# A down product between scores and state reads in every cell, the next first blocks loaded later, and two steps of y exchanged, in a fused mLSTM cell and GELU block

## The chip, the cores and the metric

The kernel runs on one core of one Trainium2 chip. The metric is the device time of one execution in microseconds (us), from which the median of several runs is taken. The engines are TensorE (PE: matmuls and transposes into PSUM, with its weight loads PEld), VectorE (DVE), ScalarE (ACT), GpSimd (POOL) and SyncE (SP, which here issues every data DMA).

## The reference

Two blocks follow each other. The first is a recurrence for batch 4, 8 heads, 768 positions and a head width of 40, cut here to what matters:

```python
for t in range(S):
    m_new = np.maximum(f_gate[:, :, t] + m, i_gate[:, :, t])
    f_stab, i_stab = np.exp(f_gate[:, :, t] + m - m_new), np.exp(i_gate[:, :, t] - m_new)
    C = f_stab * C + i_stab * outer(v[t], k[t])          # state, 40 x 40 a head
    n = f_stab * n + i_stab * k[t]
    y[:, :, t] = sigmoid(o_gate[t]) * (C @ q[t]) / max(|n . q[t]|, 1)
```

Its output, as 3072 rows of 320, goes into the second block: `h = x @ w_in` (320 x 2048), an exact GELU, and `g @ w_out` (2048 x 320). Everything is float32.

## The kernel before, in words

The 768 positions are cut into six chunks of 128 (`NCH`, `L`). For each chunk a **cell** computes the recurrence in its parallel form for the four batches b = 0 to 3: scores k·q by PE (`ps`, L505 and L521), multiplied by decay weights W that ACT makes with an exponential (L433) from a broadcast of M (loaded at L175 and L178, masked by POOL at L407); reads of the carried state (`pf`, L576), the update of the state from k and weighted v (L583, DVE and POOL around it), and the values W·v (`ph`, L615). The sum of state reads (`far`) and values is gated, divided by its denominator (`finish`, the y step, L628 to L633) and turned by PE transposes into the columns of x (`turn_y`, L650); `split_x` makes the parts that the up product wants (L668, L669). The turn reads two blocks of 128 columns from `ob` and the last 64 from `y_rest`, a copy that DVE makes at L639 (`twice`), one buffer for all batches.

The **up** stage of a chunk multiplies x by w_in in three float parts (L810, L821), and ACT applies GELU into `g` (L825). The **down** stage is `g @ w_out` in a seven-product form with sums of weights and of hidden blocks (`down_steps`): 14 steps F, each of 16 recorded matmuls at L886. Steps 1 and 2 are `p1`, 3 and 4 `p6`, 5 and 6 `p2`, 7 and 8 `p5`, 9 and 10 `p7`, 11 and 12 `p3`, 13 and 14 `p4`; after each second one ACT copies or DVE adds the bank into the output tile (L899), and `p3` and `p4` send it out (L853).

The order of the work is written out by hand. Chunk 0 and cells 0 and 1 are in a list FRONT. Then, for c = 1 to 5, the up stage of chunk c is followed by its down stage, in which cell c+1 runs; the text calls this **stage c**. The order inside it is the list DOWN for c = 1 to 3, LAST_CELL for c = 4 (DOWN with the two passes changed), and 14 plain F for c = 5. The letters: M mask, W weights, G gate, S `scores_two` (two batches), C `carry_two` (state reads and update), V values, Y finish, X `turn_y`, R `split_x`, L and B loads for the last batch, K and Q `turn_k` and `turn_q`, D its weighted values, F one down step, Z one step of the weight sums of chunk 1, N the late hidden sums (L916). Each engine executes its own instructions in the order in which the list issues them; S, C and V of two batches are called a **pass** here, so each stage has two.

In cells 2 and later k and q come as small 32 x 32 blocks, 16 loads for one batch (`load_blocks`, L158), into one buffer `blocks`, and DVE transposes them (L456). A batch's blocks are loaded when those of the batch before it are turned:

```python
def turn_q(self, b):
    self.turn_half(b, 1)
    n = self.c * B + b + (1 if b < B - 2 else 2)
    if b < B - 1 and n < NCH * B:
        load_blocks(n, by_block)
```

so Q2 loads the first batch of the next cell; the fourth batch has its own buffer inside `g`. K0, Q0, K1 and Q1 of the next cell are issued inside the next up stage. The values of a batch then issue the loads of M (L178), k and v (L146, L148) for a later one, and `turn_y` that of the o gate (L148). SP issues all of these in list order, and waits where a buffer isn't free.

## Time and profile before

| | us |
|---|---|
| median of 3 runs | 484.55 |
| the runs | 481.93, 484.55, 487.79 |
| the profiled execution | 484.29 |
| its span, first to last instruction | 482.5 |
| PE busy | 472.3 (98%) |
| PEld busy | 412.2 (85%) |
| DVE busy | 345.2 (72%) |
| ACT busy | 222.2 (46%) |
| POOL busy | 70.7 (15%) |
| down stages 1, 2, 3 and 4 | 43.7, 46.4, 43.8, 41.8 |

Times inside the kernel are counted from the first instruction. The stages are read as stretches of the timeline: 158.2 to 201.9, 230.6 to 277.0, 305.7 to 349.5 and 378.2 to 420.0. Stage 4 has less work than the others, as the last cell doesn't update the state (no L583). A float32 matmul shows as two records. Matmuls are pipelined and their ends are modelled, so lengths of PE work are best taken from start to start. "issue" names time in which an engine waited for nothing that the profile shows.

### The profile page before, as it was taken

To read this page: it belongs to the slowest core of one execution; us is meant where nothing else is said; L and a number is where in the kernel's file an instruction comes from. 1 tells how busy PE (TensorE), PEld (TensorE's weight loads), DVE (VectorE), ACT (ScalarE), POOL (GpSimd) and SP (SyncE) were. 2 spreads that over 40 slices of the span, in tenths; PEclk is the share of its full clock that TensorE was granted. 3 is DMA by queue.
4 is the path that set the end of the run, shared out by engine and by line. 5 is a ranking of instruction groups with operands and counts; after the bars stand their busy time and mean duration, and the time that the engine had idled before them with its cause. 6 is when DMAs were issued, how large, how long until landed. Compare 5 with 4: busy or idle time off the path is not lost.

```text
span 482.5 us, 11952 instructions
## 1 busy us (share of the span) xinstructions
PE 472.3 (98%) x4740; PEld 412.2 (85%) x4740; DVE 345.2 (72%) x762; ACT 222.2 (46%) x477; POOL 70.7 (15%) x104
## 2 busy tenths in 40 slices
PE   8899999999999999999998999999999999999997
PEld 7787888877777999977998977899977899977997
DVE  7899689797879898747596767398867488724321
ACT  6977999844532941122941104862104862112300
POOL 3001210000020233200333200135100114000000
PEclk9999999999999999999998999999999999999999
DMA  9998966379320364931264921255931250100001
GB/s 174 201 216 179 188 170 151 84 192 208 113 29 6 39 123 66 205 71 17 34 133 63 201 53 21 33 95 95 197 70 19 33 88 8 46 10 0 1 1 54
DMA packets 170423, 44.49 MB, mean 92 GB/s; under 512 B 156448, under 2 KB 163904, under 8 KB 170368
## 3 DMA queue, kind: packets, MB, share of 16 engines
q1 hardware_dynamic: 170368, 43.73, 46.6%
q8 instruction: 37, 0.61, 0.5%
q14 instruction: 18, 0.15, 0.1%
HBM read 39.58 MB, written 4.13 MB: 91 GB/s over the span
## 4 chain that ended last, share of the span: by engine, by line
PE 88%; DVE 6%; SPq 1%; ACT 1%; DMA 1%; issue 1%; DVEq 0%
PE po L886 31%; PE pu L810 21%; PE po L863 7%; PE pu L755 6%; PE pu L821 6%; PE ph L615 5%; PE ps L521 2%; PE pu L761 2%; PE pf L576 2%; PE px L650 2%; PE pf L583 1%; PE ps L505 1%; SPq L148 1%; PE pt L479 1%; ACT g L825 1%
## 5 line engine op out<-in xcount | busy, mean ns | idle before, releaser
L886 PE MATMUL po<-w_out,g 128*128 128x160 f32 x640 | 91.3, 300 | 0.0
L886 PEld LDWEIGHTS po<-w_out,g 128*128 128x128 f32 x640 | 87.8, 190 | 1.9 <-ACT g L825 1.8
L825 ACT ACTIVATE g<-pu 128x512 f32<-128x512 f32 x80 | 40.8, 614 | 53.4 <-PE pu L821 53.3
L886 PE MATMUL po<-w_sums,sums 128*128 128x160 f32 x320 | 48.7, 307 | 0.0
L886 PEld LDWEIGHTS po<-w_sums,sums 128*128 128x128 f32 x320 | 45.5, 195 | 0.5
L660 ACT ACTIVATE x_hi<-px 128x384 fp32r<-128x384 f32 x20 | 9.8, 489 | 69.3 <-PE px L650 69.3
L810 PE MATMUL pu<-x_hi,w_in_hi 128*128 128x512 f32 x160 | 41.7, 402 | 0.0
L742 DVE TENSOR_TENSOR sums<-g 128x512 f32<-128x512 f32 x20 | 13.8, 689 | 38.6 <-ACT g L825 38.6
L810 PE MATMUL pu<-x_lo,w_in_lo 128*128 128x512 f32 x160 | 40.6, 395 | 0.0
L433 ACT ACTIVATE W<-W,aT 128x128 f32<-128x128 f32 x128 | 39.2, 388 | 0.1
L810 PEld LDWEIGHTS pu<-x_hi,w_in_hi 128*128 128x128 f32 x160 | 28.5, 188 | 9.3 <-ACT g L825 4.1
L810 PEld LDWEIGHTS pu<-x_lo,w_in_lo 128*128 128x128 f32 x160 | 30.1, 188 | 7.2
L863 PE MATMUL po<-w_out,g 128*128 128x320 f32 x128 | 35.2, 433 | 0.0
L863 PEld LDWEIGHTS po<-w_out,g 128*128 128x128 f32 x128 | 24.0, 190 | 9.5
L810 PE MATMUL pu<-x_all,w_in_mid 128*128 128x512 f32 x80 | 31.7, 396 | 0.1
L825 ACT ACT_TABLE_LOAD x5 | 6.4, 1283 | 55.1 <-PE pu L821 41.3
L810 PE MATMUL pu<-x_all,w_mid 128*128 128x512 f32 x80 | 31.7, 396 | 0.0
L899 DVE TENSOR_TENSOR o_sb<-po,o_sb 128x320 f32<-128x320 f32 (+1 forms) x27 | 12.5, 463 | 25.9 <-PE po L886 21.9
L407 POOL TENSOR_SCALAR_AFFINE_SELECT W<-W 128x1024 f32<-128x1024 f32 (+2 forms) x20 | 21.9, 1103 | 61.7 <-DMA W<-M_d 54.2
L755 PE MATMUL pu<-first_x,w_in 128*128 128x256 f32 x128 | 29.1, 382 | 0.0
L445 POOL MEMSET g<- 32x1024 f32 x8 | 7.6, 945 | 135.1 <-ACT W L433 134.8
L755 PEld LDWEIGHTS pu<-first_x,w_in 128*128 128x128 f32 x128 | 23.8, 190 | 3.4 <-DVE w_in L375 0.4
(183 smaller groups left out, 901.6 us busy)
## 6 DMA issues: line engine op xcount, KB each, us to landing
W<-M_d SPq DMA_DIRECT2D x16, 512.0 KB, 5.2
bits<-in_moe_w_in_dram SPq DMA_DIRECT2D x20, 256.0 KB, 4.3
bits<-in_moe_w_out_dram SPq DMA_DIRECT2D x16, 320.0 KB, 3.4
ob<-in_o_gate_dram SPq DMA_DIRECT2D x24, 160.0 KB, 3.8
out_dram<-o_sb SPq DMA_DIRECT2D x24, 160.0 KB, 1.9
vb<-in_v_dram SPq DMA_DIRECT2D x14, 160.0 KB, 5.1
kb<-in_k_dram SPq DMA_DIRECT2D x14, 160.0 KB, 5.2
g<-M_d SPq DMA_DIRECT2D x4, 512.0 KB, 4.5
```

Source lines behind the costliest of these rows:

```text
L407: nc.gpsimd.affine_select(out=x, in_=x, compare_op=OP.is_ge, fill=1.0e30, base=base, pattern=[[0, H], [1, x.shape[2]]], channel_multiplier=-1)
L433: nc.scalar.activation(out=W[n][:, h, :], in_=src, func=AF.Exp, scale=-1.0, bias=aT[:, self.c, r:r + 1])
L615: nc.tensor.matmul(ph[r, h, :], Pm[:, h, r], vb[turn_of(n)][:, h, :], start=True, stop=True)
L660: nc.scalar.activation(out=parts["x"][:, :, t], in_=px, func=AF.Copy, scale=PART)
L742: nc.vector.tensor_tensor(out=s1, in0=a21, in1=a22, op=OP.add)
L755: nc.tensor.matmul(banks[-1][e][:, i - i0, :], in_tile(i, x)[:, e, i % 2 * P:(i % 2 + 1) * P], first_x[:, x, t0:t1], start=(x == 0 and i = ...
L810: nc.tensor.matmul(pus[i][e], w[k][:, e, i * P:(i + 1) * P], x[:, k, :], start=(n == 0 and k == 0), stop=False, skip_group_check=True)
L821: nc.tensor.matmul(pu[e], w[r, i // 2, i % 2 * P:(i % 2 + 1) * P], x[r, NX, :], start=False, stop=(n == 2), skip_group_check=True)
L825: nc.scalar.activation(out=g.t[:, HF * e + i, :], in_=pu[e], func=AF.Gelu, scale=4097.0)
L863: nc.tensor.matmul(po[b], g.t[:, f, b * L:(b + 1) * L], w_out[:, f, :], start=(f == 0), stop=(f == NF - 1))
L886: nc.tensor.matmul(bank[at][:, i, :], lhs(j, t), rhs(j), start=(first and i == 0 and j == 0), stop=(i == n - 1 and j == HF - 1), skip_grou ...
L899: nc.vector.tensor_tensor(out=to, in0=pb, in1=x, op=OP.add)
```

## The change

Three edits of the list, and one of the code that it calls.

In DOWN the pair "F S0" becomes "S0 F", and "S2 C2 V2 V3 F" becomes "S2 F C2 V2 V3": one down step stands between the scores and the state reads in both passes. LAST_CELL, which had these two already, goes away, and stage 4 uses DOWN.

The loads of the next cell's first blocks leave `turn_q` (Q2) and become a step of their own, `j`, issued after the values V3. In stage 4 it does nothing, as before.

"Y3 X1" becomes "X1 Y3": the second turn of y is issued before the fourth y is finished, in stages 1 to 4.

```diff
 DOWN = """
-    M0 Z M1 W0 F L3 F B3 W1 Z Z F S0 K2 C0 M2 G0 G1 G2 G3 V0 V1 W2 F Q2 K3 Q3 Y0 M3 D3 F F W3 F S2 C2 V2 V3 F Z N F Y1
-    X0 R0 Y2 F F Y3 X1 R1 F X2 R2 F X3 R3 F"""
-LAST_CELL = DOWN.replace("F S0", "S0 F").replace("S2 C2 V2 V3 F", "S2 F C2 V2 V3")
+    M0 Z M1 W0 F L3 F B3 W1 Z Z S0 F K2 C0 M2 G0 G1 G2 G3 V0 V1 W2 F Q2 K3 Q3 Y0 M3 D3 F F W3 F S2 F C2 V2 V3 j Z N F Y1
+    X0 R0 Y2 F F X1 Y3 R1 F X2 R2 F X3 R3 F"""
...
         def turn_q(self, b):
             self.turn_half(b, 1)
-            n = self.c * B + b + (1 if b < B - 2 else 2)
-            if b < B - 1 and n < NCH * B:
-                load_blocks(n, by_block)
+            if b < B - 2:
+                load_blocks(self.c * B + b + 1, by_block)
             if self.c < NCH - 1 and b < B - 1:
                 self.weigh_values(b)
+
+        def load_next(self):
+            if self.c + 1 < NCH:
+                load_blocks((self.c + 1) * B, by_block)
...
-            steps = cell_steps(c + 1, "MWGTscVYXRLKQDCBS", g)
+            steps = cell_steps(c + 1, "MWGTscVYXRLKQDCBSj", g)
...
-        play("F " * 14 if c + 1 == NCH else LAST_CELL if c + 2 == NCH else DOWN, steps)
+        play("F " * 14 if c + 1 == NCH else DOWN, steps)
```

## The prediction

> **What bounds the kernel now.** I read the page first, for the engine that sets the end. These are its busy line and its chain of waits by engine.

> ```profile
> PE 472.3 (98%) x4740; PEld 412.2 (85%) x4740; DVE 345.2 (72%) x762; ACT 222.2 (46%) x477; POOL 70.7 (15%) x104
> ...
> PE 88%; DVE 6%; SPq 1%; ACT 1%; DMA 1%; issue 1%; DVEq 0%
> ```

> TensorE (PE) is the bound: 98% busy and 88% of the chain. So an edit is worth only what it changes in PE's own sequence: a hole taken away, or a costlier order of the same matmuls. Next I cut the time into the four down stages in which a cell of the recurrence runs (stage c multiplies chunk c down while cell c+1 is computed). Columns: stretch, length, PE, PEld, DVE, ACT and POOL busy, granted clock, DMA share, GB/s.

> ```profile
> 158.20:201.90 43.70, 43.24 (x687) 42.58 (x685) 37.80 (x97) 19.91 (x50) 14.62 (x19) 1.00 0.59 102
> 230.60:277.00 46.40, 44.92 (x687) 44.22 (x686) 35.04 (x80) 19.90 (x50) 15.33 (x20) 0.96 0.59 108
> 305.70:349.50 43.80, 43.28 (x687) 42.51 (x685) 35.11 (x80) 19.87 (x50) 14.96 (x18) 1.00 0.62 110
> 378.20:420.00 41.80, 41.80 (x623) 40.78 (x622) 33.66 (x76) 19.91 (x50) 9.15 (x9) 1.00 0.25 41
> ```

> Stages 1 to 3 do the same PE work (687 matmuls), yet stage 2 takes 2.6 us more than stage 3, at a lower clock. Stage 4, which already runs with a down product between scores and state reads, has no hole at all. So I followed PE through the second score pass of stage 2 in the timeline (start, length, line, tiles, count).

> ```profile
> 251.61 1.57 PE L521 MATMUL ps<-qT,kT 64*64 64x128 f32 x64
> 253.00 1.09 PE L576 MATMUL pf<-state,qT 64*64 64x41 f32 x64
> 254.03 1.13 PE L583 MATMUL pf<-vw,kb 128*64 128x41 f32 x32
> 254.98 1.11 PE L615 MATMUL ph<-vb,W 128*64 128x41 f32 x32
> 255.91 0.29 PE L615 MATMUL ph<-vb,g 128*64 128x41 f32 x2
> 257.68 1.39 PE L615 MATMUL ph<-vb,g 128*64 128x41 f32 x30 [1.48 <-issue]
> 259.00 3.79 PE L886 MATMUL po<-w_sums,sums 128*128 128x160 f32 x16
> 262.62 2.34 PE L886 MATMUL po<-w_out,g 128*128 128x160 f32 x16
> ```

> Two losses stand here: 1.48 us in which PE waited for nothing that the profile shows, and a down product of 3.79 us where its neighbour takes 2.34. The windows give the second its reason (clock 0.50), and the DMA view of two short windows (251 to 254, then 254.9 to 256.4) hints at the first.

> ```profile
> 259.00:261.80 2.80, 2.80 (x11) 2.80 (x11) 0.50 (x1) 0.00 (x0) 1.89 (x3) 0.50 0.24 26
> ...
> q1 hardware_dynamic: 1651, 0.74, 107.1%
> ...
> q8 instruction: 1, 0.02, 5.0%
> ```

> From 251 to 254 the data queue fills all 16 DMA engines (107.1%) and no instruction packet runs. The next one, 16 KB on q8, starts at 255.04 and takes 1.21 us. Since the one before it (244.50) PE had been issued 432 instructions; over the whole trace the spacing is about 256. So the fetch was some 170 instructions late, and PE ran dry at 255.97. One pass of scores (L521), state reads (L576), state update (L583) and values (L615) is about 450 instructions in 5.4 us; a down product (L886) is 32 in 2.2 us. Only in the pass can 256 instructions be used up in about 3 us.

> [...] Here PEclk is 0.50 right behind the hole, for 3.41 us from 258.37 in the trace; the idle part was only 1.48 us[...].

> **The change part by part.**

> *A down product between scores and state reads (stages 1 to 3, twice each; stage 4 has it already).* No matmul is added; PE changes over between small and dense matmuls more often. Stage 4 shows the new order:

> ```profile
> 382.72 1.57 PE L521 MATMUL ps<-qT,kT 64*64 64x128 f32 x64
> 384.22 2.44 PE L886 MATMUL po<-w_sums,sums 128*128 128x160 f32 x16
> 386.59 1.14 PE L576 MATMUL pf<-state,qT 64*64 64x41 f32 x64
> 387.66 2.06 PE L615 MATMUL ph<-vb,W 128*64 128x41 f32 x64
> ```

> Start to start, the first pass of stage 2 with its seven products is 230.56 to 251.61: 6.72 (three products) + 1.39 + 1.02 + 0.96 (L583) + 2.07 + 8.89 (four products) = 21.05 us. In stage 4 it is 4.55 + 1.50 + 2.37 + 1.07 + 1.99 + 8.90 = 20.38 without L583; with its 0.96 it is 21.34, or 21.42 with stage 2's 2.07 for the values. So the split costs 0.29 to 0.37, say 0.33 us a pass: six passes, +2.0 us. From below it could be nothing, if some is taken up elsewhere; from above 0.38, so 0 to 2.3.

> What it takes away, in this execution: in stage 1 the first values take 168.28 to 170.95 = 2.67 us with 0.46 of "issue", against 2.07: 0.60. In stage 2 the second values take 254.98 to 259.00 = 4.02 against 2.05 in stage 3: 1.97; the product behind them 3.62 start to start against 2.28: 1.34. Together 3.9 us. With the product between, the 256 instructions that ran dry in stage 2 have 2.3 us more to arrive in, against the 1.48 that were missing; in stage 1 the same[...]. The wait of the DVE for scores doesn't appear as a cost: W is multiplied (L527, 3.1 us for two cells' tiles) before the values start, today as well.

> The moved score pass waits for nothing new: it starts 2.2 us earlier, and its banks were released by the last gelu at 232.73 in stage 2, before 235.05. The second weights (ACT, done at 239.15) then hold DVE's second half by about 1 us, as stage 4 shows (0.73 idle), but the values that need it start at 242. The add of the eighth product (L899, 0.49 us) now stands ahead of the state reads' work on DVE, and its product is done by then.

> *The next first blocks loaded behind the values.* The 16 small loads leave their place after turn 2 and go behind the M, k and v loads of both values. SP's queue, stage 3 today:

> ```profile
> 325.79 7.79 SPq L158 DMA_DIRECT2D blocks<-in_k_dram  x8
> 333.68 4.91 SPq L158 DMA_DIRECT2D blocks<-in_q_dram  x8
> ```

> They take 12.7 us to issue, against 3.8 + 3.9 elsewhere, because the loads issued just before fill the engines. They cover the whole second pass. Moved, SP stands idle until the second values have been read (about 334 in stage 3, 186.4 in stage 1), spends some 5 us on M, k and v, and issues the blocks from about 339 to 352 (191 to 204 in stage 1), last landing 2.2 us later: 354 and 206. They are wanted by the DVE transposes at 356.5/357.9 and 208.9/210.3 (k, then q). Slack 3 to 4 us for the q half, more for k; DVE then idles another 1.9 us (359.4 to 361.2) before its next join. So I cost the move at nothing. What queues behind the blocks on SP are the o loads and the output sends, which end by about 357 instead of 351; the o gates are used 25 us later, the output buffers too. The gain of the move lies in the first part: no 107% under the second pass.

> *Second turn of y ahead of the fourth y (stages 1 to 4).* No work is added. The copy of the rest of y for the third turn (L639) stood behind the fourth y's four DVE steps (1.2 to 1.9 us); now it comes right after the second turn has been read. Today it is late once, in stage 3: PE went from the third turn's first transpose at 343.75 to the next product at 344.82, 1.07 us against 0.33 for a turn without a wait. That is 0.74. Next in line is the fourth turn, which needs the bank that the second split frees: 345.5 against 347.0 in stage 3, so 1.5 us to spare.

> **Sum.** 2.0 − 3.9 − 0.74 = −2.65 us. The profiled execution took 484.29 us (span 482.5), so 481.6. It lies 0.26 below the median of the runs shown, 484.55; against that median the forecast is **481.9 us**, 0.5% less. One starving of this kind is worth 3.3 us, which is also about the step between the three runs (481.93, 484.55, 487.79): likely they differ in how many they had.

> **The rivals.** (1) *Waits stay, the switches are paid: slower.* If the late fetch comes not from the blocks but from any busy data queue, the M, k and v loads that remain ahead of the second pass, or the g blocks under the first, starve PE as before; the boundary of 256 can also fall at the start of the state reads, where 330 small instructions still follow each other. [...] Then +2.0 and only the y wait gone: 484.55 + 2.0 − 0.74 = 485.8. For it: the first pass of stage 2 has a fetch 110 instructions late with no blocks on the queue. Against it: stage 4, in this order, has no hole. (2) *The split is free*, the product fills gaps of the pass: 484.55 − 4.65 = 479.9. For it: nothing but the span of runs; stage 4 speaks against it. (3) *Blocks land late.* If they land 8 us later than I reckon, each of three up stages loses 8 − 3.4 − 1.9 = 2.7 us: 481.9 + 8.1 = 490.0. For it: 8 us for 8 issues today; against it: the same backlog is already in my sum.

> **How the numbers follow.** Forecast 0.58, rivals 0.22, 0.14, 0.06. The predicted time is the forecast's. The range 479.8 to 486.8 holds the first two rivals and leaves out the third and the tails. A measurement of this kernel tells about 1% (4.8 us) from no change. Faster by over 1%, below 479.7: half of rival 2 and a little of the forecast, 0.10. Slower, above 489.4: rival 3, 0.06. Within: 0.84.

> **What would show it.** Right: PEclk 1.00 in all four stages, no "issue" hole at L615, the split order at 21.3 to 21.4 us a pass, and stages 1 to 3 at 43.7 to 44.1 us each. Right on the move: block loads from about 339 in stage 3, and no wait of the transposes (L456) in the up stages. Wrong: a hole of over 1 us at L615 or L576, half clock in a stage, or an idle DVE ahead of L456 ended by a blocks DMA.

## The result, and the profile after

The changed kernel takes 483.63 us in the median (21 runs, 482.42 to 486.84) against 484.55 (21 runs, 481.93 to 488.06). The ratio is 0.9988, with a 95% interval of 0.9968 to 1.0008: no change that can be told. Run again beside the kernel before on another chip it gave 483.56 against 483.05, ratio 1.0011 [0.9998, 1.0023]. The forecast was 481.9. The profiled execution took 483.16 us (484.29 before), its span is 481.2 (482.5).

The page's busy line of the changed kernel, and the four down stages cut from start to start of PE's work (columns as in the prediction):

```profile
PE 473.1 (98%) x4740; PEld 410.8 (85%) x4740; DVE 351.5 (73%) x762; ACT 222.2 (46%) x477; POOL 73.7 (15%) x104
...
158.20:202.80 44.60, 44.07 (x687) 42.45 (x685) 40.67 (x97) 19.94 (x50) 15.66 (x20) 1.00 0.59 102
231.58:275.62 44.04, 43.91 (x687) 42.47 (x685) 37.00 (x80) 19.94 (x50) 17.56 (x20) 1.00 0.55 99
304.40:348.12 43.72, 43.72 (x687) 42.47 (x685) 36.67 (x80) 19.94 (x50) 15.84 (x18) 1.00 0.56 98
376.92:418.58 41.66, 41.66 (x622) 40.64 (x621) 33.42 (x76) 19.92 (x50) 8.99 (x9) 1.00 0.24 41
```

Cut in the same way, the stages before were 43.60, 46.32, 43.75 and 41.67. Stage 2 lost 2.28 us, and its clock is 1.00 now. Stage 1 *grew* by 1.00. DVE and POOL are busier by 6.3 and 3.0 us although no instruction was added to them: the same work runs slower.

The second pass of stage 2 in the changed kernel's PE timeline has no hole:

```profile
252.89 1.57 PE L523 MATMUL ps<-qT,kT 64*64 64x128 f32 x64
254.39 2.44 PE L888 MATMUL po<-w_sums,sums 128*128 128x160 f32 x16
256.76 1.14 PE L578 MATMUL pf<-state,qT 64*64 64x41 f32 x64
257.83 1.13 PE L585 MATMUL pf<-vw,kb 128*64 128x41 f32 x32
258.79 1.11 PE L617 MATMUL ph<-vb,W 128*64 128x41 f32 x32
259.72 1.11 PE L617 MATMUL ph<-vb,g 128*64 128x41 f32 x32
260.76 2.44 PE L888 MATMUL po<-w_out,g 128*128 128x160 f32 x16
```

(Line numbers are those of the kernel shown; they differ by a few from kernel to kernel.) Most of what stage 1 lost stands at the second turn of y, first before, then after the change:

```profile
194.39 0.38 PE L650 MATMUL px<-ident,ob 128*128 128x128 f32 x2
194.61 0.27 PE L650 MATMUL px<-ident,y_rest 128*128 128x128 f32 x1
```

```profile
189.99 4.51 PE L888 MATMUL po<-w_out,g 128*128 128x160 f32 x32
194.47 0.41 PE L652 MATMUL px<-ident,ob 128*128 128x128 f32 x2
195.41 0.33 PE L652 MATMUL px<-ident,y_rest 128*128 128x128 f32 x1 [0.53 <-DVE y_rest L641]
```

After the change PE is ready at 194.5 and the copy `y_rest` comes at 195.4. Its maker, DVE, and POOL beside it, from their timelines; first before, then after the change:

```profile
192.13 0.49 DVE L633 TENSOR_TENSOR ob<-ob,den 128x320 f32<-128x320 f32 x1
192.73 0.23 DVE L639 COPY y_rest<-ob 128x128 f32<-128x128 f32 x1
...
199.16 0.74 POOL L492 TENSOR_TENSOR vw<-vb,ewT 128x328 f32<-128x328 f32 x1 [10.11 <-DMA vb<-in_v_dram]
199.85 2.86 POOL L407 TENSOR_SCALAR_AFFINE_SELECT W<-W 128x1024 f32<-128x1024 f32 x3
```

```profile
192.20 0.74 POOL L494 TENSOR_TENSOR vw<-vb,ewT 128x328 f32<-128x328 f32 x1 [2.32 <-DMA vb<-in_v_dram]
192.89 3.10 POOL L406 TENSOR_SCALAR_AFFINE_SELECT W<-W 128x1024 f32<-128x1024 f32 x3
...
193.30 1.02 DVE L635 TENSOR_TENSOR ob<-ob,den 128x320 f32<-128x320 f32 x1
194.43 0.93 DVE L641 COPY y_rest<-ob 128x128 f32<-128x128 f32 x1
```

Before, POOL waited 10.11 us for the next cell's v, because the block loads stood ahead of it on SP's queue. Now v comes 7 us earlier, POOL makes the weighted v and masks the next W at once, and the same two DVE instructions, which run beside that, take 1.02 and 0.93 us instead of 0.49 and 0.23. ACT, which reads these masks in the next stage, doesn't begin there until 235.07, about 39 us later.

### The profile page after: what moved, and what is told of

The parts are those of the page before. It is cut to its first block, busy times and chain, and to the rows that moved or that the text cites. A ratio compares the mean times of both kernels' runs of the same rounds, so it can differ in the third digit from the quotient of the medians.

```text
span 481.2 us, 11954 instructions
## 1 busy us (share of the span) xinstructions
PE 473.1 (98%) x4740; PEld 410.8 (85%) x4740; DVE 351.5 (73%) x762; ACT 222.2 (46%) x477; POOL 73.7 (15%) x104
## 4 chain that ended last, share of the span: by engine, by line
PE 87%; DVE 7%; ACT 1%; SPq 1%; DMA 1%; issue 1%; DVEq 0%
PE po L888 30%; PE pu L812 22%; PE po L865 7%; PE pu L757 6%; PE pu L823 6%; PE ph L617 5%; PE ps L523 2%; PE pf L578 2%; PE pu L763 2%; PE px L652 2%; PE pf L585 1%; DVE g L918 1%; PE ps L507 1%; SPq L147 1%; PE pt L481 1%; ACT g L827 1%
## 5 line engine op out<-in xcount | busy, mean ns | idle before, releaser
L888 PE MATMUL po<-w_sums,sums 128*128 128x160 f32 x320 | 47.7, 303 | 0.0
L888 PEld LDWEIGHTS po<-w_sums,sums 128*128 128x128 f32 x320 | 44.1, 190 | 0.7
```

Of the source, the lines that this page charges most:

```text
L888: nc.tensor.matmul(bank[at][:, i, :], lhs(j, t), rhs(j), start=(first and i == 0 and j == 0), stop=(i == n - 1 and j == HF - 1), skip_grou ...
```

## The experiments

Two questions were open: what had made the hole and what had taken it away, and what had made the second turn late. On the first, theory A says that in a pass PE uses up its instructions before the next packet on q8, the queue that the page calls `instruction`, has brought more (37 packets of 16 KB before, one for every 255 of PE's recorded instructions on average); its rivals are the loads under the pass, or a data wait. On the second, theory B says that POOL's work, released early by the moved loads, slows DVE; its rival is the split passes, which leave only one product, not two, between the values and the first turn. All ratios are against the kernel before, run on the same chip.

### Each part alone

The split alone (stages 1 to 3 use LAST_CELL):

```diff
-        play("F " * 14 if c + 1 == NCH else LAST_CELL if c + 2 == NCH else DOWN, steps)
+        play("F " * 14 if c + 1 == NCH else LAST_CELL, steps)
```

> The kernel before with a down step between scores and state reads in all stages; the first blocks stay after turn 2 and the fourth y stays ahead of the second turn. Theory A (the late fetch is bridged by the product alone): no hole at L615 and clock 1.00 in stages 1 to 3, a pass 0.27 us longer than before's clean one, no wait of the second turn of y in stages 1 and 2, since POOL's masks still come at about 200 in stage 1; 482.5 to 483.5. Rival (the data queue must be clear, too): a hole or half clock in the second pass of a stage as before, 484.5 or more.

Measured 482.65 against 483.13, ratio 0.9986 [0.9969, 1.0003]. No hole is left at the values although the blocks are still loaded under the second pass; stages 1 to 3 took 43.83, 43.54 and 44.74. In stage 3 the *third* turn waits:

```profile
343.32 0.38 PE L650 MATMUL px<-ident,ob 128*128 128x128 f32 x2
344.68 0.33 PE L650 MATMUL px<-ident,y_rest 128*128 128x128 f32 x1 [0.98 <-DVE y_rest L639]
```

So the product alone takes the hole away, and it lengthens the wait that the exchange of X1 and Y3 is there to remove (0.52 us at the same place in the profile before).

The move alone:

```diff
-            n = self.c * B + b + (1 if b < B - 2 else 2)
-            if b < B - 1 and n < NCH * B:
-                load_blocks(n, by_block)
+            if b < B - 2:
+                load_blocks(self.c * B + b + 1, by_block)
...
-    M0 Z M1 W0 F L3 F B3 W1 Z Z F S0 K2 C0 M2 G0 G1 G2 G3 V0 V1 W2 F Q2 K3 Q3 Y0 M3 D3 F F W3 F S2 C2 V2 V3 F Z N F Y1
+    M0 Z M1 W0 F L3 F B3 W1 Z Z F S0 K2 C0 M2 G0 G1 G2 G3 V0 V1 W2 F Q2 K3 Q3 Y0 M3 D3 F F W3 F S2 C2 V2 V3 j F Z N F Y1
```

> The kernel before with the next first blocks loaded behind the third and fourth values; order of PE unchanged. Theory A (the full data queue makes the fetch late): no hole in the second pass of stage 2, clock 1.00, about 3 us under a before with the hole, 481.5 to 482.5. POOL's masks and weighed values come some 7 us earlier and the sums N and the second y on DVE grow by 2 to 3 us, but two products stand between the values and the first turn, so the second turn waits by less than 0.2 us. Rival (256 small instructions in 3 us starve PE whatever the queue does): the hole stays, 484.5.

Missed on the hole and on the turns: 486.52 against 483.13, ratio 1.0065 [1.0046, 1.0083]. The hole stays in stage 2 without any block load under it, and in stage 1 the second and third turns wait:

```profile
257.80 0.29 PE L618 MATMUL ph<-vb,g 128*64 128x41 f32 x2
259.83 1.13 PE L618 MATMUL ph<-vb,g 128*64 128x41 f32 x30 [1.74 <-issue]
...
195.00 0.41 PE L653 MATMUL px<-ident,ob 128*128 128x128 f32 x2 [0.69 <-DVE ob L636]
198.94 0.33 PE L653 MATMUL px<-ident,y_rest 128*128 128x128 f32 x1 [0.98 <-DVE y_rest L642]
```

The move doesn't empty the data queue: the loads of M, k and v that remain ahead of the second pass fill it, at 107.0% of the engines in the 3.4 us up to the packet on q8. The changed kernel's own packet on q8 there, at 256.20, has the same 107.0% ahead of it.

The exchange alone:

```diff
-    X0 R0 Y2 F F Y3 X1 R1 F X2 R2 F X3 R3 F"""
+    X0 R0 Y2 F F X1 Y3 R1 F X2 R2 F X3 R3 F"""
```

> The kernel before with the second turn of y issued ahead of the fourth y. Both theories: only the wait of the third turn (0.74 us in stage 3) can go, the holes of the second pass come and go as before: 484.0 to 484.5, same within 0.2%. If the exchange itself made the second turn late, stages 1 and 2 would show 0.3 to 0.8 us at L650 ahead of the second turn.

482.58 against 483.13, ratio 0.9995 [0.9969, 1.0020]. The hole is there (1.25 us of "issue" at 256.89), this time with no half clock behind it: the product after it takes 2.44 us, not 3.79. Stage 3, which has neither hole nor wait, took 43.02.

### The changed kernel with one part undone

> The changed kernel with the fourth y ahead of the second turn again (split and move kept). Theory B: the second turn waits in stages 1 and 2 as in the changed kernel, and the third turn now too, behind the fourth y, by 0.5 to 1.2 us in stages 1 to 3; span 1.5 to 3 us over the changed kernel. Rival (the exchange is worth nothing): within 0.3 us of the changed kernel, stages 1 to 3 unchanged.

```diff
-    X0 R0 Y2 F F X1 Y3 R1 F X2 R2 F X3 R3 F"""
+    X0 R0 Y2 F F Y3 X1 R1 F X2 R2 F X3 R3 F"""
```

486.53 against 483.23, ratio 1.0054 [1.0038, 1.0071]; stages 45.99, 45.08 and 44.75. The third turn waits about 1 us in all three, the second 0.77 in stage 1. Beside the move the exchange is worth 2 to 3 us (1.0054 against 1.0011 or 0.9988 for the changed kernel); alone it is worth nothing that can be told.

> The changed kernel with the next first blocks loaded behind turn 2 again (split passes and exchanged turn kept). Theory B (the move brings POOL's work for the next cell under DVE's sums and second y): POOL's masks back at about 200 in stage 1, N 2.35 us in stages 1 and 2, no wait of the second turn, stages 1 to 3 at 43.5 us each as with POOL held; span about 1.3 us under the changed kernel. Theory A (the product bridges the late fetch alone): no hole at L615's place although the blocks lie under the second pass. Rival (the move is what keeps the second pass free): a hole of 1 us or more and half clock in stage 2.

```diff
-            if b < B - 2:
-                load_blocks(self.c * B + b + 1, by_block)
+            n = self.c * B + b + (1 if b < B - 2 else 2)
+            if b < B - 1 and n < NCH * B:
+                load_blocks(n, by_block)
...
-    M0 Z M1 W0 F L3 F B3 W1 Z Z S0 F K2 C0 M2 G0 G1 G2 G3 V0 V1 W2 F Q2 K3 Q3 Y0 M3 D3 F F W3 F S2 F C2 V2 V3 j Z N F Y1
+    M0 Z M1 W0 F L3 F B3 W1 Z Z S0 F K2 C0 M2 G0 G1 G2 G3 V0 V1 W2 F Q2 K3 Q3 Y0 M3 D3 F F W3 F S2 F C2 V2 V3 Z N F Y1
```

481.35 against 483.23, ratio 0.9953 [0.9933, 0.9973]. The stages, from its windows:

```profile
158.19:201.72 43.53, 43.53 (x686) 42.52 (x685) 38.94 (x97) 19.93 (x50) 15.17 (x20) 1.00 0.59 103
230.50:274.04 43.54, 43.54 (x687) 42.52 (x685) 35.63 (x80) 19.94 (x50) 17.35 (x20) 1.00 0.58 102
302.82:346.48 43.66, 43.66 (x686) 42.48 (x685) 36.43 (x80) 19.93 (x50) 16.21 (x18) 1.00 0.62 109
```

No hole, no wait, blocks where they were. In one detail the expectation missed: N still takes 2.89 to 3.18 us, as POOL's gating of y (1.79 us at 260.52 in stage 2), in stage 1 its weighing of v (0.81 us at 189.05), runs beside it; what came back is the second y and its copy (0.49 and 0.23 us). On this run's page DVE and POOL are busy for 348.4 and 73.6 us, against 345.2 and 70.7 before: half of DVE's growth and nearly all of POOL's are there without the move.

### Is it POOL?

The move is kept, and POOL made to wait (`h`, at the end of DOWN, behind R3):

```diff
+    def hold_pool():
+        nc.vector.memset(hold, 0.0)
+        nc.gpsimd.memset(hold, 0.0)
```

> The changed kernel with one small memset on DVE behind the last split of x and one on POOL that waits for it, so that POOL's weighed values and masks of the next cell run after the y steps and not under them. Theory B (POOL beside it slows DVE's sums and second y, and so the copy for the second turn): N back from 2.9 to 3.2 to 2.35 us, the y_rest copy back to 0.23, no wait of the second turn in stages 1 and 2, span 1.2 to 1.5 us under the changed kernel: 482.0. Rival (the moved product alone leaves DVE too little time): the waits of 0.3 to 0.8 us stay, 483.2 or more.

481.43 against 483.13, ratio 0.9968 [0.9950, 0.9986]; stages 43.53 each. POOL, DVE and the second turn on PE in stage 1:

```profile
204.50 0.10 POOL L965 MEMSET hold<- 128x1 f32 x1 [12.38 <-DVE hold L964]
...
195.20 0.49 DVE L635 TENSOR_TENSOR ob<-ob,den 128x320 f32<-128x320 f32 x1
195.79 0.23 DVE L641 COPY y_rest<-ob 128x128 f32<-128x128 f32 x1
...
197.35 0.38 PE L652 MATMUL px<-ident,ob 128*128 128x128 f32 x2
197.57 0.27 PE L652 MATMUL px<-ident,y_rest 128*128 128x128 f32 x1
```

The order of the loads is the changed kernel's, and the waits are gone. So it is POOL's work beside DVE, not the order of the loads itself, and not the shorter time that the split leaves: theory B holds. N fell to 2.35 only in stage 1 (3.17 in stages 2 and 3), for the reason given above.

### Is it the instruction blocks?

The kernel before, with its instruction count shifted by 144 by tiny matmuls at the start:

```diff
+    shift = ps_h.tile([P, P], F32, name="shift", tag="h")
+    for _ in range(36):
+        nc.tensor.matmul(shift[0:32, 0:32], w_out[:, 0, 0:32], w_out[:, 0, 0:32], start=True, stop=True, skip_group_check=True)
```

> The kernel before with 36 tiny extra matmuls (144 PE instructions) at its start, which write a bank that nothing reads. Theory A (blocks of 256 instructions run dry in a pass of about 455 when their boundary lies in the first 200): the hole leaves the second pass of stage 2, whose boundary moves from 116 to 228 behind its start, and stands in the second passes of stage 1 (97) and stage 3 (71), and in first passes of stage 1 (171), 2 (48) or 3 (148). Rival (a data or DVE wait at that place, or the data queue alone): the hole stays in the second pass of stage 2. The total is some us longer by the extra matmuls and by one or two holes.

488.13 against 483.23, ratio 1.0093 [1.0065, 1.0121], the extra matmuls included. The hole left the second pass of stage 2 and stands in the second passes of stages 1 and 3 and in the first of stage 2, in this order:

```profile
186.75 1.48 PE L618 MATMUL ph<-vb,g 128*64 128x41 f32 x32 [1.67 <-DMA blocks<-in_k_dram]
...
335.26 0.48 PE L618 MATMUL ph<-vb,W 128*64 128x41 f32 x9 [1.02 <-issue]
...
247.07 1.16 PE L618 MATMUL ph<-vb,W 128*64 128x41 f32 x33 [0.99 <-DMA g<-in_k_dram]
```

The two loads named here are ones that the values don't read; they are what happened to land last. Two first passes that the count also allowed, of stages 1 and 3, had no gap over 0.24 us between two matmuls. Data, loads and their order are the same; the count differs, and the first down stage starts 1.4 us later. A wait on data would have stayed with the values that it belongs to.

The traces settle it more sharply than the windows of the expectation. Number PE's recorded instructions (weight loads, matmuls and the few others) from 0 in order of their start. The hole in the second pass of stage 2 ends at number 5313 in all four kernels with the old count: before, the move alone, the exchange alone, and the last kernel of this section; the smaller one in stage 1 of the profile before ends at 3009. With 144 instructions more the holes end at 3777, 4801 and 7105, with 48 more (next run) at 3777 and 7105. Each of these numbers is a multiple of 256 plus 193: when the count shifts, the holes leave the matmuls that they stood at and stay on this grid. In each of them PE goes on 2.3 to 2.9 us after the packet of q8 ahead of it started (257.68 against 255.04 in stage 2 before). That PE waits for this packet is what I conclude from the two; no wait in the profile names it. The distance in instructions between packets, by which the prediction called a fetch 170 late, doesn't tell: in the profile before packets 365 and 382 instructions behind the last (at 240.29 and 183.93) left no hole.

The same on the held kernel, by 48:

```diff
-    for _ in range(36):
+    for _ in range(12):
```

> The changed kernel with POOL held behind the last split of x, and 12 tiny extra matmuls (48 PE instructions) at its start. Theory A: in the split order only the state reads, update and values (about 327 instructions) still run without a product, so a boundary 160 to 231 behind a pass's start starves PE; the shift puts three there (second pass of stage 1 at 193, first of stage 2 at 176, second of stage 3 at 167), so two or three holes of 0.3 to 1.5 us where the unshifted kernel had none, stages 1 to 3 up from 43.5 by that. Rival (the split cures the starving wherever the boundary lies): all three stages stay at 43.5.

483.73 against 483.23, ratio 1.0011 [0.9984, 1.0037]. Two of the three places named have a hole, and stages 1 and 3 rise from 43.53 to 44.93 and 44.94:

```profile
189.53 0.26 PE L620 MATMUL ph<-vb,g 128*64 128x41 f32 x2 [1.15 <-issue]
...
335.27 0.55 PE L620 MATMUL ph<-vb,g 128*64 128x41 f32 x11 [1.17 <-issue]
```

The first pass of stage 2 has none, and the stage takes 43.53. So the split is no cure for every count: the profiles of the changed kernel show no hole at the values, and with 48 more there are two.

And what does a full data queue add? The kernel with the move alone, without the k and v loads ahead of stage 2's second pass:

```diff
-            if self.c > 1 and self.reads.count(b) == 2:
+            if self.c > 1 and self.reads.count(b) == 2 and not (self.c == 3 and b < 2):
```

> As the kernel with only the blocks moved, and in cell 3 the loads of k and v that follow the values of the first two batches are left out (stale tiles are used), so that the data queue is nearly empty ahead of the late fetch of stage 2. If a full queue is what delays the fetch: it comes about 1 us earlier, and the hole in the second pass of stage 2 shrinks from 1.97 between two matmuls to 0.4 to 0.8. If PE's own pace is all (a block of 256 in about 3 us): the hole stays at 1.5 to 2.

The hole shrank from 1.74 to 0.39 us of "issue" (1.97 to 0.62 between the two matmuls), with the engines 44.1% busy and not 107.0% in the 3.4 us before the packet on q8. Both theories were half right at this place: 0.4 to 0.6 is left without the full queue, which I put down to PE's pace, and the full queue costs 1.3 more (one profile of each). Elsewhere more is left without it: the hole of 0.99 us at 247.07 in the kernel with 144 more instructions had the engines only 34.6% busy in the 3.4 us before its packet. (484.96 in all, two runs, with POOL's waits of the move in it.)

```profile
258.18 0.29 PE L618 MATMUL ph<-vb,g 128*64 128x41 f32 x3
258.85 1.07 PE L618 MATMUL ph<-vb,g 128*64 128x41 f32 x29 [0.39 <-issue]
...
q1 hardware_dynamic: 175, 0.60, 44.1%
```

### The comparison on one chip

The changed kernel, then split and exchange without the move, then that with POOL held:

> The changed kernel itself once more, on the chip of the next three. Both theories: no hole at the values, waits of the second turn in stages 1 and 2 of 0.3 to 0.8 us, 482.5 to 483.5.

> Split passes and exchanged turn with the first blocks behind turn 2, on the same chip as the changed kernel. Theory B: 1.2 to 2 us under the changed kernel, 481.0 to 481.6. Rival (the earlier gap between the two came from the chips): within 0.5 us of it.

> Split passes and exchanged turn, first blocks behind turn 2, and POOL held behind the last split of x. Theory B: POOL's masks leave stage 3's y steps too, so stages 1 to 3 at 43.53 us each, no better than the kernel without the hold by more than 0.2 us: 481.0 to 481.5. Rival (the hold makes POOL late for the next cell's weights): a stage over 43.6 or ACT late at L433's place, 482 or more.

Against 483.05 for the kernel before: changed 483.56, 1.0011 [0.9998, 1.0023]; without the move 481.28, 0.9969 [0.9955, 0.9983]; without it and POOL held 481.25, 0.9969 [0.9954, 0.9984]. The version without the move (6 runs) beats both kernels, by 1.8 and 2.3 us; holding POOL on top of it adds nothing. The two profiles show 1.3 of the 2.3 us (spans of 480.8 and 479.5), most of it in stages 1 and 2; the changed kernel's profiled execution was one of its faster ones, and where the others lose the rest no trace shows.

## Why the prediction was wrong, point by point

**Right: the bound, the fetch, the split.** PE is the bound (98% busy in both profiles), the hole goes with PE's instruction count and not with its data (the shift by 144), and the product between scores and state reads bridges it (1.48 us before, none in the split alone). Its price was over-estimated: 43.53 for a stage with the split against 43.02 for a clean one without, so 0.51 a stage or 0.26 a pass, not 0.33; over six passes 1.5 us instead of 2.0. The kernel without the move shows the sum of split and exchange: its stages 1 to 3 took 130.73 us against 133.67 in the profile before, −2.9, where the prediction had −2.65. That this is so close is in part luck, as the profile before had the half clock: in the medians split and exchange together gain 1.8 and 1.9 us (483.05 to 481.28 and 483.23 to 481.35).

**Wrong: the move "at nothing".** This is the step that failed. The slack of the moved loads was right: no transpose waited, and they were issued from 189.8 to 200.5 in stage 1, for which I had 191 to 204. What I left out is what they moved *past*. I counted the M, k and v loads as a delay for the blocks and didn't ask what their earlier landing would release. The list of waits had it: POOL waited for `vb`, up to 10.1 us at a time, and that wait kept its weighing and masks out of DVE's y steps. I had also seen the fourth y's DVE steps take "1.2 to 1.9 us" and taken the spread as given; the slow ones in stage 3 (1.23 us for the product, 0.68 for the copy) stood beside POOL's masks (342.57 to 344.52), too. What the two engines get into each other's way over no run shows: the product, which reads two tiles, slows (0.49 to 1.02 us), and the copy, which reads one, slows too (0.23 to 0.93). On one chip the move costs 483.56 − 481.28 = 2.3 us, which eats what the other two edits gain.

**Wrong in part: what the move gains.** "No 107% under the second pass" didn't happen: the loads that remain fill the queue (107.0% in the move alone and in the changed kernel). That was rival 1's mechanism. Its number, 485.8, was not that of the changed kernel, which has no hole there all the same, as it has the split (the product from 254.39 to 256.76).

**Mis-sized: the half clock.** I counted its 1.34 us as part of every execution. The exchange's profile shows the hole without it. Of the 172 runs of the kernel before beside the experiments, 59 had a granted clock at or below 0.996; on the last chip the medians with and without were 484.81 and 482.78. The profile before was one of the first kind. But the clock of a whole run doesn't say where its half clock fell. In the profiles of the split alone and of POOL held, both at 0.996 but at 1.00 in all four down stages, it is the 3.41 us from 15.7 and 15.4 us on, long before stage 1, and 12 of the 43 runs of the changed kernel were at or below 0.996, too. So the steps between the three runs, which I put down to "one starving of this kind", are of a size that the half clock alone can make (484.43 for POOL held's profiled run, whose median is 481.43); how many of them belong to the hole stays open.

**Right on the exchange,** though for a larger reason than I gave: with the split the third turn waits 0.98 us in stage 3 without it, and with the move it waits in every stage.

## What to carry to other kernels

When loads change places on a queue, follow those that come *earlier* as carefully as those that come later: find who waits for them now, and what that engine will do, and beside whom, once it no longer waits. A wait on an idle engine can be what keeps it out of the way of a busy one, as POOL's 10.11 us did here. And where PE has a gap in a stretch of very small matmuls with no wait named, number its recorded instructions before looking for data: here the gaps of 0.39 to 1.74 us ended at multiples of 256 plus 193, and 144 or 48 more instructions moved them to other matmuls.
